# Normalized attention and a feed-forward block on one core: the first group's normalization in parts, two k scalings split over two engines, and two loads and two activations moved in their queues

## Chip, core, metric

One Trainium2 chip; the kernel runs on one of its cores. The metric is the device time of one execution in microseconds, as the median of several runs.

## What is computed

q, k and v have 8 batches, 12 heads, 448 tokens and a head dimension of 64, in float32. The attention output, 3584 tokens by 768, goes through an up-projection to 2048, a leaky activation with a slope per feature, and a down-projection to 768.

```python
def rmsnorm(x, g):
    rms = np.sqrt(np.mean(x * x, axis=-1, keepdims=True) + 1e-06)
    return x / rms * g
q_n, k_n = (rmsnorm(q, g_q), rmsnorm(k, g_k))
scores = (1.0 / np.sqrt(64)) * np.matmul(q_n, k_n.transpose(0, 1, 3, 2))
attn = softmax(scores)                       # over the keys
x = np.matmul(attn, v)                       # heads side by side: 3584 x 768
h = x @ w_in                                 # 3584 x 2048
g = np.maximum(h, 0.0) + alpha * np.minimum(h, 0.0)
out = g @ w_out                              # 3584 x 768
```

## The kernel before

A *group* `y` is one batch's four heads out of twelve: three groups to a batch (`G = 3`), 24 in all. Its q and k come as two tiles `nat` of 128 x 896 float32 (two halves of the heads on the two halves of the partitions; along a partition two heads `h`, seven token blocks `j` and 64 elements). Six such tiles exist, so three groups can be in the core at once. A group then goes through these steps:

- `load_qk` (L97): two DMAs for q and two for k, on SP's queue (half of those of groups 0 and 1 on ScalarE's).
- `square` (L141), on ScalarE for groups 0 and 1 and on GpSimd (POOL) after; `reduce` (L151), on VectorE; `root` (L159), two small ScalarE operations that make 1/rms; `scale` (L168), q or k times 1/rms, on VectorE for k of group 0 and q of groups 1 to 3 and on POOL for all others.
- `turn` (L188): for groups 0 to 5 fourteen TensorE transposes (`tps`) and two copies out of PSUM, `qT` and `kT`, the latter with the gains; from group 6 on two DMA transposes on SP's queue (`turn_dma`, L178) and only the gain on VectorE (L192).
- `score` (L225) and `soft` (L243), for each of the seven key blocks of a group: four or eight matmuls into one of two double banks `sc`, and one exponential of 128 x 896 on ScalarE, 1.0 us, into `expT`.
- `den`, `log`, `invert` and `attv`: the sums over the keys, their reciprocals by logarithm and exponential on ScalarE, the product with v, and `xT` on VectorE.

The feed-forward block is cut into pieces too. `up(b, ft)` (L344) makes one of 16 feature tiles of a batch: six matmuls into a PSUM bank `hT`, a ScalarE copy times the slope (`ah`, L354) and a VectorE maximum (`gT`, L355), which releases the bank. `down` (L357) is a chain of 16 matmuls into a bank `op`, a VectorE copy `osb` (L377) and two output DMAs on SP's queue. Feature tiles 0 to 3 of batch 0 are begun before the last third of the batch's attention is there (`begin`, L335): 0 and 1 in two single banks, 2 and 3 in the two halves of one shared tile (`hTb`).

The order of everything is written by hand: each engine runs its instructions in the order in which the program emits them. A list of *bursts* of two or three score tiles is laid out first; for every burst `n` the lists `prep`, `jobs`, `post` and `roots` say which loads, reduces, squares and roots go with it, `turns` which group is turned at it, and `gaps` which `up` and `down` pieces follow its scores. Burst `den_at[G - 1]`, the `lead`, is the one in which the attention of batch 0 ends and its up-projection starts; there `root` and `scale` of group 4 come after four `up` pieces. `spin` (L390) is a filler matmul whose result nobody reads; it keeps TensorE busy where it would wait. POOL's queue also issues the loads of v, w_in and w_out, among its squares and scales; w_out comes in four chunks of 768 KB. In the start, SP's queue issues groups 0 to 2 at once; groups 8 and 9 are loaded four bursts ahead of their reduces.

Of the kernel before, what the change touches and what calls it, by code (L numbers as in the profile page):

```python
# [9 lines left out]
FP32 = mybir.dt.float32  # L10
# [11 lines left out]
def kernel(  # L22
# [118 lines left out]
    def square(y, nm):  # L141
        src = nat[y, nm].rearrange("p h j d -> p (h j d)")
        sq = ld.tile([128, 2 * J, D], FP32, name="sq", tag="sq", bufs=4)
        sqf = sq.rearrange("p n d -> p (n d)")
        if y < 2:
            nc.scalar.activation(out=sqf, in_=src, func=AF.Square)  # L146
        else:
            nc.gpsimd.tensor_mul(out=sqf, in0=src, in1=src)  # L148
        sqs[y, nm] = sq

    def reduce(y, nm):  # L151
        if nm == "q":
            ss_t[y] = ld.tile([128, 2, 2, J], FP32, name="ss", tag="ss", bufs=4)
        nc.vector.tensor_reduce(  # L154
            out=ss_t[y][:, "qk".index(nm)].rearrange("p h j -> p (h j)").unsqueeze(2),
            in_=sqs[y, nm], axis=AXIS_X, op=ALU.add,
        )

    def root(y, nms="qk"):  # L159
        n = len(nms)  # L160
        at = "qk".index(nms[0])
        if at == 0:
            rr_t[y] = ld.tile([128, 2, 2, J], FP32, name="rr", tag="rr", bufs=4)
        rr, ss = rr_t[y][:, ds(at, n)], ss_t[y][:, ds(at, n)]
        nc.scalar.activation(out=rr, in_=ss, func=AF.Ln, scale=1.0 / D, bias=epsb[:, 0:1])
        nc.scalar.activation(out=rr, in_=rr, func=AF.Exp, scale=-0.5)

    def scale(y, nm):  # L168
        t = ld.tile([128, J, 2, D], FP16, name="qs", tag="qs", bufs=4)
        eng = nc.vector if (y, nm) in ((0, "k"), (1, "q"), (2, "q"), (3, "q")) else nc.gpsimd  # L170
        eng.tensor_mul(  # L171
            out=t.rearrange("p j h d -> p h j d"),
            in0=nat[y, nm],
            in1=rr_t[y][:, "qk".index(nm)].unsqueeze(3).broadcast_to((128, 2, J, D)),
        )
        qs[y, nm] = t

    def turn_dma(y):  # L178
        for nm in "qk":
# [8 lines left out]
    def turn(y):  # L188

        if y >= TD:  # L190
            t = qkT[y, "k"].rearrange("p j g c -> p (j g c)")
            nc.vector.tensor_scalar(  # L192
                out=t, in0=t, scalar1=gain[:, 0:1], scalar2=None, op0=ALU.mult
            )
            return
        if y <= G:
            ps = [psf.tile([128, 512], FP32, name="tps", tag="mm") for _ in "qk"]
        else:
            ps2 = psa.tile([128, 2, 512], FP32, name="tps2", tag="acc")
            ps = [ps2[:, 0], ps2[:, 1]]  # L200
        tps = [
            t[:, : S].bitcast(FP16).rearrange("p (j c) -> p j c", j=J) for t in ps
        ]
        for tp, nm in zip(tps, "qk"):
            for j in range(J):
                nc.tensor.transpose(  # L206
                    tp[:, j, :], qs[y, nm][:, j].rearrange("p h d -> p (h d)"), ident
                )
        for tp, nm in zip(tps, "qk"):
            t = att.tile([128, J, 2, 64], FP16, name=f"{nm}T", tag=f"{nm}T", bufs=4)  # L210
            o = t.rearrange("p j g c -> p j (g c)")
            if nm == "q" and y == 0:
                nc.scalar.copy(out=o, in_=tp)
            elif nm == "q":
                nc.vector.tensor_copy(out=o, in_=tp)
            else:
                nc.vector.tensor_scalar(
                    out=o, in0=tp, scalar1=gain[:, 0:1], scalar2=None, op0=ALU.mult
                )
            qkT[y, nm] = t  # L220
# [114 lines left out]
    def begin(ft):  # L335
# [5 lines left out]
            begun[2], begun[3] = t[:, 0], t[:, 1]  # L341
        up_part(begun[ft], 0, ft, 0, G - 1)

    def up(b, ft, spare=False):  # L344
        if b == 0 and ft in begun:
            hT = begun[ft]

            for n in {2: (2, 3), 3: ()}.get(ft, (ft,)):
                up_part(begun[n], 0, n, G - 1, G)
        else:  # L350
            hT = bank("hT", spare)
            up_part(hT, b, ft, 0, G)
        ah = ffn.tile([128, S], FP16, name="ah", tag="ah", bufs=3)
        nc.scalar.activation(out=ah, in_=hT[:, :S], func=AF.Copy, scale=alpha_sb[:, ft : ft + 1])  # L354
        nc.vector.tensor_max(out=gT[:, ft, ds((b & 1) * S, S)], in0=hT[:, :S], in1=ah)  # L355

    def down(b0, t, oh, jobs=(), spare=False):  # L357

# [31 lines left out]
    def spin(count, wide=True):  # L390

        ps = psf.tile([128, 512], FP32, name="spin", tag="mm")
        for _ in range(count):
            nc.tensor.matmul(  # L394
                out=ps[:, :S], lhsT=idle32[:, :128] if wide else ident,
                rhs=idle32 if wide else idle, start=True, stop=True,
            )
# [10 lines left out]
    m = 0  # L408
# [32 lines left out]
                last_in[y] = n  # L441
            m += 1
    NB = len(bursts)
    prep, post, roots = {}, {}, {}

    def at(n, f, *a):
        prep.setdefault(max(int(n), 0), []).append((f, a))
# [12 lines left out]
    for y in range(G, NG):  # L460

        early = y < G + 2
        if early:
            n = turn_at[y - 1] + 1
        elif y == G + 2:
            n = den_at[G - 1]
        elif y == 2 * G:
            n = turn_at[y] - 4
        elif y % G == 1:
            n = den_at[y - 4] - 1  # L470
        elif y % G:
            n = den_at[y - G]
        else:
            n = av_at[y - 4]
        at(n - (6 if early else 4 if y <= 3 * G else 5), load_qk, y)
        for nm in "qk":
            if y != 2 * G:
                after(n - 2, square, y, nm)
            if early:
                after(n, reduce, y, nm)  # L480
            else:
                jobs.setdefault(n, []).append((reduce, (y, nm)))
        roots[n + 1] = y
    for b in range(1, B):
        at(av_at[G * b] - 6, load_v, b)
# [87 lines left out]
    load_qk(1, True)  # L573
    load_qk(2)

    spin(3)
    spin(17, False)
    ct = psf.tile([128, 512], FP32, name="ct", tag="mm")
    nc.tensor.transpose(ct[:, : NF + 2], rows, ident32[: NF + 2, : NF + 2])
    spin(1)  # L580
    for nm in "qk":
        square(0, nm)
        reduce(0, nm)
    nc.vector.tensor_copy(out=cols, in_=ct[:, : NF + 2])
    for nm in "qk":
        root(0, nm)
        scale(0, nm)
    nc.vector.tensor_mul(
        out=gain, in0=cols[:, NF : NF + 1], in1=cols[:, NF + 1 : NF + 2]
    )  # L590
    square(1, "q")
    turn(0)
    square(1, "k")
    load_v(0)
    square(2, "q")
    for nm in "qk":
        reduce(1, nm)
    after(0, root, 1)
    for nm in "qk":
        after(0, scale, 1, nm)  # L600
    after(0, square, 2, "k")
    after(0, load_w_in, 0)
    for nm in "qk":
        after(2, reduce, 2, nm)
    after(5, load_w_in, 1)
    after(7, load_w_in, 2)
    after(8, load_w_in, 3)
# [1 line left out]
        after(first + (0, 0, 2, 4)[c], load_w_out, c)  # L609
    for nm in "qk":  # L610
        after(first, square, 2 * G, nm)
    roots[3] = 2

    since = 2
    for n in range(NB):
# [4 lines left out]
        lead = n == den_at[G - 1]  # L620
        first_tiles = tiles[: 2 if lead else split.get(n, 2)]
        for t in first_tiles:
            score(*t)
            if n == den_at[G - 1] - 1 and t == tiles[-1]:
                begin(0)
                begin(1)
            elif lead and t == tiles[0]:
                soft(*t)
                den(dens[n])
                attv(avs[n], 0, True, (log, invert))  # L630
            elif lead and t == tiles[1]:
                begin(2)
        plain = lead or n not in dens and n not in avs
        wait = plain and not lead and gaps[n] and gaps[n][0][0] is up
        if lead:
            begin(3)
        for t in tiles[:1] if wait else tiles[1:2] if lead else first_tiles:
            soft(*t)
        if n in dens and not lead:
            den(dens[n])  # L640
# [15 lines left out]
        if n in roots:  # L656
            y = roots[n]
            work = [(root, (y,)), (scale, (y, "q")), (scale, (y, "k"))]
            if lead:

                late = [(2, score, tiles[2]), (2, soft, tiles[2])]
            if lead or wait and y < TD:
                late += [(4 if lead else 1, f, a) for f, a in work]
            else:
                for f, a in work:
                    f(*a)
            if y >= TD:
                turn_dma(y)
# [28 lines left out]
        for k, (f, a) in enumerate(gaps[n]):  # L697
            spare = k in spare_at
            if f is down:
                down(*a, jobs.pop(n, ()), spare)  # L700
            else:
                f(*a, spare)
                done += 1
                if n in jobs and not (lead and done < 4):
                    g, c = jobs[n].pop(0)
                    g(*c)
                    if not jobs[n]:
                        del jobs[n]
                while late and done == late[0][0]:
                    _, g, c = late.pop(0)  # L710
                    g(*c)
        if not gaps[n] and n in turns:
            turn(turns[n])
        for _, g, c in late:
            g(*c)
# [36 lines left out]
```

## Time and profile before

| | |
|---|---|
| median of 6 runs | 433.4 us (431.95 to 434.43) |
| the profiled execution | 433.73 us, of which the span of its trace is 431.9 us |
| TensorE (PE), loads of its weights (PEld) | busy 417.1 and 216.3 us |
| ScalarE (ACT), VectorE (DVE), GpSimd (POOL) | busy 279.0, 203.2 and 175.2 us |
| DMA | 53.85 MB moved, 125 GB/s over the span |
| exponential `expT`, 168 of them | 1004 ns each |
| POOL `qs` and `sq`, 44 each | 1761 and 1677 ns each |
| VectorE `ss` (reduce), 48 of them | 1077 ns each |

Busy time is the sum of an engine's instructions. TensorE's includes the fillers. Where the text gives a moment (13.43), it is in microseconds from the start of the span.

### The profile page before, as it was taken

How to read it: one execution, taken by the hardware profiler on the slowest of the kernel's cores; microseconds unless marked ns; L12 is line 12 of the kernel's file. 1: busy time of each engine (PE TensorE's matmuls, PEld its weight loads, DVE VectorE, ACT ScalarE, POOL GpSimd, SP SyncE). 2: the span in 40 equal slices, each digit the busy share in tenths (PEclk: the TensorE clock that was granted, in tenths of full speed). 3: DMA queues.
4: the chain of work that ended last, by engine and by line, in shares of the span. 5: the costliest groups of instructions: out<-in, count | busy, mean ns of one | idle time of the engine just before them, and what ended most of it. 6: DMA issues, size and time to landing. Idle time of an engine off the chain costs nothing.

```text
span 431.9 us, 11487 instructions
## 1 busy us (share of the span) xinstructions
PE 417.1 (97%) x4964; PEld 216.3 (50%) x4964; DVE 203.2 (47%) x304; ACT 279.0 (65%) x385; POOL 175.2 (41%) x133
## 2 busy tenths in 40 slices
PE   8789899899999999999999999999999999999996
PEld 3344344454455445544555445544555445555564
DVE  3755764455545463545444463545453353233421
ACT  4997888677976677767667577757757577132300
POOL 5799696393184407380283506371163000000000
PEclk9999999999999999999999999999999999999999
DMA  8999899999669824878059833774073300211133
GB/s 195 235 220 219 154 212 147 241 192 212 129 109 193 180 80 63 171 146 185 20 96 196 174 115 61 152 149 116 20 119 87 77 1 21 56 38 32 24 73 75
DMA packets 70387, 53.85 MB, mean 125 GB/s; under 512 B 37424, under 2 KB 70336, under 8 KB 70336
## 3 DMA queue, kind: packets, MB, share of 16 engines
q1 hardware_dynamic: 55536, 40.19, 43.0%
q0 software_dynamic: 13984, 11.81, 19.1%
q10 hardware_dynamic: 816, 1.11, 1.1%
q8 instruction: 39, 0.64, 0.6%
q14 instruction: 12, 0.10, 0.1%
HBM read 45.62 MB, written 11.01 MB: 131 GB/s over the span
## 4 chain that ended last, share of the span: by engine, by line
PE 86%; ACT 5%; DMA 4%; DVE 3%; POOL 1%; issue 1%
PE op L365 27%; PE hT L327 21%; PE hTa L327 11%; PE sc L232 7%; PE opa L365 6%; PE av L261 4%; PE dn L261 4%; DMA w_out_sb<-in_moe_w_out_dram 4%; ACT expT L246 3%; PE spin L394 2%; PE avb L261 2%; DVE ss L154 1%; PE tps L206 1%; DVE gT L355 1%; POOL sq L148 1%; DVE osb L377 1%
## 5 line engine op out<-in xcount | busy, mean ns | idle before, releaser
L246 ACT ACTIVATE expT<-sc,expb 128x896 f16<-128x896 f32 x168 | 161.5, 1004 | 36.8 <-PE sc L232 35.8
L171 POOL TENSOR_TENSOR qs<-nat,rr 128x896 f16<-128x896 f32 x44 | 76.7, 1761 | 148.6 <-issue 79.0
L365 PE MATMUL op<-w_out_sb,gT 128*128 128x384 f16 (+1 forms) x752 | 126.5, 323 | 1.0 <-DMA w_out_sb<-in_moe_w_out_dram 1.0
L365 PEld LDWEIGHTS <-gT 128*128 128x128 f16 x912 | 85.8, 98 | 66.6 <-issue 14.0
L327 PEld LDWEIGHTS <-w_in_sb 128*128 128x128 f16 x768 | 73.2, 98 | 75.8 <-issue 11.5
L327 PE MATMUL hT<-xT,w_in_sb 128*128 128x448 f16 x510 | 107.1, 353 | 2.8 <-DVE gT L355 2.2
L354 ACT ACTIVATE ah<-hT,cols 128x448 f16<-128x448 f32 x85 | 53.7, 634 | 44.6 <-PE hT L327 44.6
L355 DVE TENSOR_TENSOR gT<-hT,ah 128x448 f16<-128x448 f32 x85 | 52.8, 623 | 51.0 <-ACT ah L354 51.0
L148 POOL TENSOR_TENSOR sq<-nat 128x896 f32<-128x896 f32 x44 | 72.9, 1677 | 9.3 <-DMA nat<-in_q_dram 6.8
L377 DVE COPY osb<-op 128x384 f32<-128x384 f32 (+1 forms) x47 | 25.8, 548 | 86.7 <-PE op L365 86.7
L232 PE MATMUL sc<-qT,kT 64*32 64x448 f16 (+1 forms) x1092 | 53.2, 356 | 4.3 <-ACT expT L246 2.8
L154 DVE TENSOR_REDUCE ss<-sq 128x14 f32<-128x896 f32 x48 | 50.5, 1077 | 9.5 <-ACT sq L146 5.9
L327 PE MATMUL hTa<-xT,w_in_sb 128*128 128x448 f16 x246 | 53.2, 352 | 0.0
L354 ACT ACTIVATE ah<-hTa,cols 128x448 f16<-128x448 f32 x41 | 26.0, 634 | 31.3 <-PE hTa L327 31.3
L355 DVE TENSOR_TENSOR gT<-hTa,ah 128x448 f16<-128x448 f32 x41 | 25.6, 623 | 26.0 <-ACT ah L354 26.0
L232 PEld LDWEIGHTS <-kT 64*32 64x32 f16 (+1 forms) x1092 | 15.0, 93 | 36.2 <-issue 30.8
L365 PE MATMUL opa<-w_out_sb,gT 128*128 128x384 f16 x160 | 27.7, 326 | 0.6 <-DVE xT L312 0.6
L312 DVE TENSOR_TENSOR xT<-av,rden 128x896 f16<-128x896 f32 x16 | 17.4, 1090 | 17.9 <-PE av L261 14.2
L261 PEld LDWEIGHTS <-vt 64*32 64x32 f16 (+1 forms) x1260 | 18.9, 94 | 13.2 <-issue 2.2
L261 PE MATMUL dn<-expT,ones 64*32 64x448 f16 (+1 forms) x812 | 24.2, 350 | 0.9
L261 PE MATMUL av<-expT,vt 64*32 64x448 f16 (+1 forms) x812 | 24.1, 349 | 0.0
L278 ACT ACTIVATE rden<-dn 128x896 f32<-128x896 f32 x16 | 14.5, 907 | 7.3 <-PE dn L261 7.3
(45 smaller groups left out, 160.7 us busy)
## 6 DMA issues: line engine op xcount, KB each, us to landing
out_dram<-osb SPq DMA_DIRECT2D x109, 96.0 KB, 2.3
nat<-in_q_dram SPq DMA_DIRECT2D x46, 224.0 KB, 5.4
nat<-in_k_dram SPq DMA_DIRECT2D x46, 224.0 KB, 6.7
vt<-in_v_dram POOLq DMA_DIRECT2D x16, 336.0 KB, 6.9
w_in_sb<-in_moe_w_in_dram POOLq DMA_DIRECT2D x12, 256.0 KB, 8.1
w_out_sb<-in_moe_w_out_dram POOLq DMA_DIRECT2D x4, 768.0 KB, 12.4
nat<-in_q_dram ACTq DMA_DIRECT2D x2, 224.0 KB, 4.9
nat<-in_k_dram ACTq DMA_DIRECT2D x2, 224.0 KB, 6.2
```

What stands on the lines that cost most here:

```text
L148: nc.gpsimd.tensor_mul(out=sqf, in0=src, in1=src)
L154: nc.vector.tensor_reduce(out=ss_t[y][:, "qk".index(nm)].rearrange("p h j -> p (h j)").unsqueeze(2), in_=sqs[y, nm], axis=AXIS_X, op=ALU.add,)
L171: eng.tensor_mul(out=t.rearrange("p j h d -> p h j d"), in0=nat[y, nm], in1=rr_t[y][:, "qk".index(nm)].unsqueeze(3).broadcast_to((128, 2, ...
L232: nc.tensor.matmul(out=sc[ds(64 * g + m * c, m), par, :S].rearrange("p (j c) -> p j c", j=J), lhsT=kT[ds(64 * par, 64), j, g, ts(c, m)], r ...
L246: nc.scalar.activation(out=expT[y][:, j], in_=scs[y, j][:, :, :S], func=AF.Exp, scale=QK_SCALE, bias=expb[:, 0:1],)
L261: nc.tensor.matmul(out=accs[g][ds(m * h, m), :S], lhsT=weights(g, y, par, ts(c, m), j), rhs=expT[y][ds(64 * g, 64), j, par, :], start=(j = ...
L312: nc.vector.tensor_mul(out=x, in0=av[:, :, :S], in1=r)
L327: nc.tensor.matmul(out=hT[:, :S], lhsT=w_in_sb[:, g * G + i, ts(ft, 128)], rhs=xT[b][:, g, i, :], start=(i == 0 and g == 0), stop=(i == G ...
L354: nc.scalar.activation(out=ah, in_=hT[:, :S], func=AF.Copy, scale=alpha_sb[:, ft : ft + 1])
L355: nc.vector.tensor_max(out=gT[:, ft, ds((b & 1) * S, S)], in0=hT[:, :S], in1=ah)
L365: nc.tensor.matmul(out=ops[c][:, :PW], lhsT=gT[:, ft, ts(t, 128)], rhs=w_out_sb[:, ft, ds(oh * OH + c * PW, PW)], start=(ft == 0), stop=(f ...
L377: nc.vector.tensor_copy(out=o[:, ts(c, PW)], in_=ops[c][:, :PW])
```

## The change

- The first group. `square`, `reduce`, `root`, `scale` and `turn` of group 0 are written out in parts: q is squared and reduced head by head (2 x 448), with one root and one scale on POOL; k is squared, reduced, rooted, scaled on VectorE, transposed and copied in token blocks 0 to 2 and 3 to 6. The scores of the first blocks stand ahead of the transposes of the others. The copy `qT` of this group moves from ScalarE to VectorE; one filler ahead of the first transposes goes and one at the start.
- Groups 1 and 2. The square of group 1's k moves from ScalarE to POOL. `root` and `scale` move to just before the last exponential of bursts 1 and 4, and the scaling of k is split by heads, one half on VectorE and one on POOL. The turns of both groups move to just ahead of scores (1,0) and (1,6), which is one tile later than before.
- The shared tile. `ah` and `gT` of feature tiles 2 and 3 of batch 0 are held until those of tile 4 have been emitted. In the lead, `root` and `scale` of group 4 come after two `up` pieces and not four; the second reduce of group 5 goes to the next burst's list.
- Loads. Groups 8 and 9 are loaded after burst `den_at[3]`; on SP's queue they come behind two outputs, the transposes of group 7 and two more outputs, where they came ahead of all of these.

```diff
     def scale(y, nm):
         t = ld.tile([128, J, 2, D], FP16, name="qs", tag="qs", bufs=4)
-        eng = nc.vector if (y, nm) in ((0, "k"), (1, "q"), (2, "q"), (3, "q")) else nc.gpsimd
+        eng = nc.vector if nm == "q" and 0 < y <= G else nc.gpsimd
...
+    def part_scale(nm, j, n, eng, y=0, h=None):
+        if (y, nm) not in qs:
+            qs[y, nm] = ld.tile([128, J, 2, D], FP16, name="qs", tag="qs", bufs=4)
+        hs, m = (slice(0, 2), 2) if h is None else (slice(h, h + 1), 1)
+        eng.tensor_mul(
+            out=qs[y, nm][:, j, hs].rearrange("p j h d -> p h j d"),
+            in0=nat[y, nm][:, hs, j],
+            in1=rr_t[y][:, "qk".index(nm), hs, j].unsqueeze(3).broadcast_to((128, m, n, D)),
+        )
...
+        if b == 0 and ft in (2, 3):
+            held.append((hT, ft))
+            return
+        units = [(hT, ft)]
+        if b == 0 and ft == 4:
+            prelu(units, b)
+            units = held
+        prelu(units, b)
...
-        at(n - (6 if early else 4 if y <= 3 * G else 5), load_qk, y)
+        if y in (2 * G + 2, 3 * G):
+            after(den_at[G], load_qk, y)
+        else:
+            at(n - (6 if early else 4 if y <= 3 * G else 5), load_qk, y)
...
-                jobs.setdefault(n, []).append((reduce, (y, nm)))
+                jobs.setdefault(n + (y == G + 2 and nm == "k"), []).append((reduce, (y, nm)))
...
-    spin(3)
+    spin(2)
     spin(17, False)
...
-    spin(1)
-    for nm in "qk":
-        square(0, nm)
-        reduce(0, nm)
+    K0 = 3
+    both, full, lo, hi = slice(0, 2), slice(0, J), slice(0, K0), slice(K0, J)
+    for h in range(2):
+        part_square("q", slice(h, h + 1), full, nc.scalar)
+    for h in range(2):
+        part_reduce("q", slice(h, h + 1), full)
+    part_root("q", full)
+    part_scale("q", full, J, nc.gpsimd)
+    part_square("k", both, lo, nc.scalar)
+    part_square("k", both, hi, nc.scalar)
+    part_reduce("k", both, lo)
+    part_reduce("k", both, hi)
+    part_root("k", lo)
+    part_scale("k", lo, K0, nc.vector)
+    part_root("k", hi)
+    square(1, "q")
     nc.vector.tensor_copy(out=cols, in_=ct[:, : NF + 2])
...
+    part_turn("q", range(J))
+    part_turn("k", range(K0))
+    part_copy("q", full, nc.vector)
+    part_copy("k", lo, nc.vector)
+    load_v(0)
     square(1, "k")
-    load_v(0)
+    part_scale("k", hi, J - K0, nc.vector)
+    reduce(1, "q")
     square(2, "q")
+    after(0, part_turn, "k", range(K0, J))
+    after(0, part_copy, "k", hi, nc.vector)
+    after(0, reduce, 1, "k")
+    mid[1] = 1
...
-    roots[3] = 2
+    mid[4] = 2
...
+            if t in ((1, 0), (1, J - 1)):
+                turn(1 + (t[1] > 0))
             score(*t)
...
+            if n in mid and t == tiles[-1]:
+                root(mid[n])
+                scale(mid[n], "q")
+                part_scale("k", full, J, nc.vector, mid[n], 0)
+                part_scale("k", full, J, nc.gpsimd, mid[n], 1)
             soft(*t)
...
-                late += [(4 if lead else 1, f, a) for f, a in work]
+                late += [(2 if lead else 1, f, a) for f, a in work]
```

## The prediction

> **What bounds the kernel now.** I read the 40 slices first, for which engine is full where; then the waits, for what stops TensorE; then the chain in order of time; then the timeline around each place that the change touches.
>
> ```profile
> PE   8789899899999999999999999999999999999996
> ...
> ACT  4997888677976677767667577757757577132300
> ...
> PEclk9999999999999999999999999999999999999999
> DMA  8999899999669824878059833774073300211133
> ```
>
> A slice is 10.8 us. From the tenth on TensorE is full, so there a microsecond is won only by removing matmuls, and the change removes none of those that compute. Time is to be had in the first nine slices. There PE's digits still flatter it, since its fillers (spin, L394) count as busy. In the windows from 0 to 100 us PE is idle 10.4 us in all; from 100 to 300 us it is idle 0.6 us. DMA is full nearly throughout those first nine slices as well.
>
> ```profile
> PE hT L327 <- DVE gT L355: 2.2, 2, 1.7
> ...
> PE op L365 <- DMA w_out_sb<-in_moe_w_out_dram: 1.0, 1, 1.0
> ```
>
> Two of TensorE's waits after the start: it waits for VectorE to release an up-projection bank (the 1.7 us one at 49.0) and for the last chunk of w_out (at 86.3). The chain shows what comes before:
>
> ```profile
> 12.25 0.70 DVE kT L217
> 12.95 0.04 issue
> 12.99 0.41 PE sc L232 x4
> 13.40 0.02 issue
> 13.43 1.91 ACT expT L246 x2
> ...
> 17.64 0.38 PE sc L232 x4
> 18.02 0.51 PE tps L206 x7
> 18.54 0.02 issue
> 18.56 0.62 DVE qT L215
> 19.18 0.63 DVE kT L217
> ...
> 67.86 18.40 DMA w_out_sb<-in_moe_w_out_dram
> 86.27 0.04 issue
> 86.31 1.46 PE op L365 x8
> ```
>
> The first exponential starts at 13.43. From there to 36.6 ScalarE is the bound: sixteen exponentials at a step of 0.91 us (two take 1.91 with the tail of the last), with roots of 0.48 between them, and one gap of 0.47 at 21.4. Only two score banks exist, so a score waits for the exponential two before it.
>
> **What the Trainium skill says.** "SBUF — State Buffer", section "Who interferes with whom": a VectorE instruction with two SBUF inputs and a GpSimd one that reads SBUF exclude each other. The trace agrees: POOL's scale takes 1.69 us at 8.95 and 2.59 at 15.87, where VectorE's 1.09 us scale starts at 15.83. "DMA: Bandwidth & Descriptors", section "Queues, rings and completion order": each DMA engine goes round the queues packet by packet, so SP's loads slow POOL's. The trace agrees: the last w_out chunk takes 18.4 us to land beside loads and transposes, another one 9.1. "TensorE: Matmul & The Clock Gate", section "What's actually happening": an idle window of about 3.4 us halves the clock. The trace shows 1.00 throughout and no idle stretch of that length; no run here shows the other case.
>
> **Part 1, the first group.** Now: q lands at 5.52; square 0.95, reduce 1.09; q's root waits behind k's square and ends at 8.87; POOL's scale ends at 10.64; k's side ends with kT at 12.95. After, the durations of the halves are interpolated between the 14-element root (0.21) and the 896-element square (0.95): half a square 0.58, half a reduce 0.58.
> - q: squares 5.52 to 6.56, the second reduce ends at 7.2, root (0.54) 7.76, ahead of k's square. POOL's scale (1.69) 7.84 to 9.53, 1.1 earlier. One spin fewer before it and none behind ct let PE take it at once.
> - k: squares 7.76 to 8.85 in two parts; reduces to 8.83 and 9.5; root of tokens 0 to 2 at 9.40; their scale on VectorE to 10.05; cols and gain to 10.35; qT, now on VectorE instead of ScalarE, 0.62 to 10.98; kT of three token blocks (0.68 x 3/7 = 0.3) to 11.3; score 11.35; first exponential about 11.8.
> - So 1.6 us earlier. ScalarE also loses the copy (0.91) and the square of k of group 1 (0.95), both of which stood before 13.43. That square goes to POOL behind v's two DMA issues (1.37): 10.9 to 12.6; its reduce ends at 14.6, root at 15.1. Behind it on POOL wait group 2's squares and w_in's issues; their users (21.8 and 35.1 before) have slack.
>
> **Part 2, turns one tile later.** Group 1's transposes stood behind score (0,5); now they stand behind (0,6). From the end of the exponential that frees that score's bank to the first exponential of group 1 the trace of before takes 2.7 us (17.60: score 0.38, transposes to 18.56, qT, kT to 19.81, score, 20.30). Before, three exponentials cover it (2.7); after, two (1.8). New gap 0.9. A spin (0.95 from issue to the next score) now stands between (1,0) and (1,1): another 0.35. The gap of 0.47 goes, since the reduces end before ScalarE asks. The same at group 2's turn, with the spin before (2,0): 0.5. Scaling k by halves (VectorE 0.6 beside POOL 0.85 instead of 1.69 on POOL, stretched to 2.59) brings qs from 18.46 to about 17.4, but the transposes wait for score (0,6) anyway: worth nothing on its own. Sum: 1.6 - 0.9 - 0.35 + 0.47 - 0.5 is 0.3; followed tile by tile (root of group 3 at 29.2 against 29.64) it is 0.4. I take 0.4; the ends are 0 and 1.6 (turns hidden).
>
> **Part 3, shared-tile outputs later.** Feature tile 4 goes through ScalarE and VectorE ahead of 2 and 3. Its gT ends at 46.8 instead of 48.99, and the 1.7 us wait at 49.04 goes. Late next: gT of 2 and 3 to 47.95, group 5's first reduce (1.08) to 49.0, gT 5 to 49.6, the second reduce to 50.6, the root in order on ScalarE to 51.15, ah 6, gT 6 at 52.4 (51.77 before). Tile 8 needs that bank: it ends at 53.7 against 54.0. So 0.3 of the 1.7 is kept (ends 0 and 1.7). The root of group 4 comes 1.7 earlier, and POOL, back to back from 47.4 to 68.8, moves forward; w_out's last issue goes from 67.86 to about 66.5.
>
> **Part 4, loads of groups 8 and 9 later.** On SP the eight loads (1.83 MB) leave the place behind group 6's transposes (68.3 to 77.9) and come behind two outputs, group 7's transposes and two more outputs. What they stood beside speeds up: group 6's kT lands at 77.27 now and holds VectorE, behind it xT, behind that the bank for PE at 78.77 (0.61). And w_out's chunk, 18.4 us now, takes 9 to 12 as the others: landed at about 77, needed at 85: the 1.01 goes. Sum 1.6. The cost: group 7's transposes start when its scale ends (74) and issue by 77; two outputs; the loads issue from about 78 to 83 and land (1.83 us each at the 250 GB/s of this stretch) at 82.5, 84.8, 86.7, 88.5, against 80.15, 84.1, 86.8 and before 88.5 now. VectorE waits in order for their squares, with an output copy, kT and xT behind. I price that at nothing within the slack, 0.6 us as worked out under the third rival, and at up to 4 without it.
>
> **The rest.** Two spins fewer: filler; from 8.6 to 9.5 PE stands idle, far under the window named above; 0 to 1 us. Group 5's second reduce a burst later: already in the order above. From 100 us on nothing moves but the start.
>
> Sum: 0.4 + 0.3 + 1.6 = 2.3. The profiled execution took 433.73 (span 431.9, 1.8 around it), 0.3 above the median of 433.4. 433.73 - 2.3 is 431.4; set against the median, **431.1**.
>
> **Rivals.**
> 1. *The turns cost nothing* (0.2): the whole 1.6 of the first group survives and more of the 1.7. For it: group 1's scaled k is ready early. Against: the order on PE is fixed, and (1,0) can't run before kT. 1.6 + 0.6 + 1.6 = 3.8: 429.6.
> 2. *Head and lead gain nothing, and the transfers bind* (0.22): DMA is full from 2 to 48 us, the earlier v load (POOL at 9.5 instead of 10.6) delays group 2's q, on which POOL already waits to 13.54, and the turns eat the rest. Only part 4 stays, less late loads: 0.8: 432.6.
> 3. *Slower: group 8's k lands late* (0.14). VectorE takes reduce q, reduce k, output copy (0.56), kT (0.45 to 0.70), xT (1.07) in order; PE needs that xT at 92.93 - 2.3 = 90.6, so the reduce must end by 88.3, and nat k must land by 85.5 (square 1.68, reduce 1.09): 0.6 us after my 84.8. Each microsecond beyond is lost. Issued at 80, it loses when it takes over 5.5 us; all such loads have a median of 5.8 and here they reached 14.4. At 9.5 us it costs 4: 433.4 + 4 - 2.3 = 435.1.
>
> **How the numbers follow.** The case of the sum has 0.44; it gives 430 to 432.1. About 0.3% (1.3 us) is what a measurement of this kernel can tell from no change. Faster by more, under 432.1: the sum's case and the first rival, with a little of the second, 0.67. Within it: most of the second and the near end of the third, 0.2. Slower, over 434.7: 0.13. The range leaves out 0.1 below and 0.1 above: 428.8 to 434.6.
>
> **What would show it.** After: first exponential at 11.8; ScalarE idle near 19 for about 0.9 and near 27 for 0.4; group 3's root at about 29.2; no PE wait of 1.7 us before the seventh up tile but one of about 1 for the ninth; qT and kT of group 6 landed before VectorE asks; no op wait for w_out; VectorE's reduce of group 8 waiting for POOL near 85 and PE not. The prediction is wrong if the head's 1.6 arrives whole at 30 us, or if PE waits for xT or an output bank near 90.

## The result and the profile after

The changed kernel takes 434.55 us (median of 35 executions, 431.88 to 439.52); the kernel before, beside it, 433.48 us (72 executions). The ratio is 1.0018, with a 95% interval of 1.0003 to 1.0033: no gain, and a small loss. Executions more than 1.5% above the fastest of their kernel are left out of all ratios and of the table by clock below; they are few, except where POOL issues group 8's loads, with nine of 22 (438.4 to 444.4 us; of the kernel before, beside it, two of 27). The profiled execution took 435.54 us, its span 433.4, against 433.73 and 431.9 before.

Most of the parts went as the sum has them, and TensorE stood 2.5 us ahead at 85 us. At 105 us it was 1.6 us behind. First the slices of the changed kernel, the same rows as before:

```profile
PE   8789899979999999999999999999999999999996
...
ACT  5898888758877577758757577757757577132300
...
PEclk9999999989999999999999999999999999999999
DMA  8999999999559743788049742775064300211133
```

One digit in each of two rows tells the story. The ninth slice, 87 to 98 us, now has a 7 on PE and an 8 for the granted clock; before, the clock had 9 in all forty slices. The waits of the changed kernel (engine, line and tile, what it waited for: us in total, times, the longest):

```profile
DVE ss L154 <- POOL sq L148: 8.6, 3, 5.7
...
PE sc L294 <- DVE kT L256: 2.3, 1, 2.3
...
PE hT L389 <- DVE gT L418: 1.2, 2, 0.8
```

TensorE's waits for w_out and for an up-projection bank of 1.7 us are gone from the list. A new one of 2.3 us stands in it, on VectorE's kT, and above it what VectorE was waiting for: POOL's squares, which stood waiting for their loads. The chain in order of time (start, us, what) shows how these hang together:

```profile
80.86 7.23 DMA nat<-in_k_dram
...
88.24 1.69 POOL sq L148
...
90.96 0.55 DVE osb L458
...
92.32 0.57 PE sc L294 x8
92.89 2.36 PE hT L389 x6
95.25 1.68 PE hTa L389 x6
...
104.86 1.24 PE hT L389 x6
106.10 1.14 PE hTa L389 x6
```

Group 8's k is issued at 80.86 and lands at 88.08. Then come POOL's square, VectorE's reduce (to 91.04) and, behind that reduce in VectorE's order, the output copy, kT of group 7, and only then the score. The two lines after the score cost a second time: the same groups of six matmuls that take 1.24 and 1.14 us at 105 took 2.36 and 1.68 here. Windows of two microseconds (length, busy time of PE, PEld, DVE, ACT and POOL with counts, granted clock, DMA share, GB/s) show why:

```profile
90.00:92.00 2.00, 0.00 (x0) 0.00 (x0) 2.00 (x3) 0.54 (x2) 1.66 (x2) 1.00 1.08 289
92.00:94.00 2.00, 1.68 (x12) 0.65 (x13) 2.00 (x3) 1.01 (x1) 2.00 (x3) 0.71 1.07 221
94.00:96.00 2.00, 2.00 (x7) 0.83 (x6) 1.72 (x3) 0.68 (x3) 2.00 (x3) 0.50 0.87 150
```

TensorE is empty for 2.33 us, to 92.32, and the clock then falls to a half. Idle 2.33 and slow matmuls 1.66 (2.36 + 1.68 less 1.24 + 1.14) make 4.0 of the 4.1 us between "2.5 ahead" and "1.6 behind". From 150 to 420 us the windows of both kernels agree.

In the head, three of ScalarE's exponentials (start, us, in brackets the idle time before and what ended it):

```profile
19.51 1.01 ACT L308 ACTIVATE expT<-sc,expb 128x896 f16<-128x896 f32 x1 [0.88 <-PE sc L294]
20.77 1.01 ACT L308 ACTIVATE expT<-sc,expb 128x896 f16<-128x896 f32 x1 [0.26 <-PE sc L294]
...
27.07 1.91 ACT L308 ACTIVATE expT<-sc,expb 128x896 f16<-128x896 f32 x2 [0.34 <-PE sc L294]
```

The first exponential, not shown, starts at 11.60 instead of 13.43, 1.83 us earlier. The turns of groups 1 and 2 give back the 0.88, 0.26 and 0.34 shown here, as a turn one tile later has to. And in the lead TensorE's timeline has two new gaps where the wait of 1.7 us was:

```profile
48.17 0.38 PE L294 MATMUL sc<-qT,kT 64*64 64x448 f16 x4 [0.90 <-ACT expT L308]
...
51.34 1.30 PE L389 MATMUL hT<-xT,w_in_sb 128*128 128x448 f16 x6 [0.77 <-DVE gT L418]
```

### The profile page after: what moved, and what is told of

Its sections match the earlier page's. It is cut to its first block, busy times and chain, and to the rows that moved or that the text cites. A ratio compares the mean times of both kernels' runs of the same rounds, so it can differ in the third digit from the quotient of the medians.

```text
span 433.4 us, 11492 instructions
## 1 busy us (share of the span) xinstructions
PE 417.1 (96%) x4960; PEld 216.4 (50%) x4960; DVE 206.5 (48%) x311; ACT 278.3 (64%) x387; POOL 176.3 (41%) x134
## 4 chain that ended last, share of the span: by engine, by line
PE 83%; ACT 5%; DVE 4%; issue 2%; POOL 2%; DMA 2%; SPq 1%; ACTq 1%; POOLq 0%
PE op L446 26%; PE hT L389 22%; PE hTa L389 11%; PE sc L294 7%; PE opa L446 6%; PE dn L323 4%; PE av L323 4%; ACT expT L308 2%; PE avb L323 2%; DMA nat<-in_k_dram 2%; DVE ss L154 1%; DVE gT L418 1%; DVE osb L458 1%; POOL qs L171 1%; POOL sq L148 1%
## 5 line engine op out<-in xcount | busy, mean ns | idle before, releaser
L171 POOL TENSOR_TENSOR qs<-nat,rr 128x896 f16<-128x896 f32 x41 | 69.6, 1719 | 140.9 <-issue 93.2
L148 POOL TENSOR_TENSOR sq<-nat 128x896 f32<-128x896 f32 x45 | 75.7, 1703 | 12.6 <-DMA nat<-in_q_dram 10.2
L154 DVE TENSOR_REDUCE ss<-sq 128x14 f32<-128x896 f32 x46 | 48.5, 1077 | 8.6 <-POOL sq L148 8.6
```

The costliest lines, as they stand in the source:

```text
L154: nc.vector.tensor_reduce(out=ss_t[y][:, "qk".index(nm)].rearrange("p h j -> p (h j)").unsqueeze(2), in_=sqs[y, nm], axis=AXIS_X, op=ALU.add,)
L171: eng.tensor_mul(out=t.rearrange("p j h d -> p h j d"), in0=nat[y, nm], in1=rr_t[y][:, "qk".index(nm)].unsqueeze(3).broadcast_to((128, 2, ...
```

## The experiments

In the expectations, A is the theory that the late landing of group 8's k is what the change pays for. B, as its rival, says that what is won early is lost again whatever the loads do. D is the theory that the new start puts the granted clock at risk, so that its gain arrives only in part of the executions. Ratios are to the kernel before, run on the same chip. The changed kernel was not run again beside these, so a comparison with it goes over two ratios.

### A: taking the late loads away, and having nothing but them

**Loads back at their place, the rest of the change kept:**

```diff
-        if y in (2 * G + 2, 3 * G):
-            after(den_at[G], load_qk, y)
-        else:
-            at(n - (6 if early else 4 if y <= 3 * G else 5), load_qk, y)
+        at(n - (6 if early else 4 if y <= 3 * G else 5), load_qk, y)
```

> The changed kernel with the loads of groups 8 and 9 back in their old place on SP's queue. Theory A (late k: VectorE waits in order for group 8's k, TensorE then stands 2.3 us idle near 90 us and runs about 1.7 us slow behind it): both losses go, the start's 1.5 us stays won, w_out's last chunk is waited for again (1.0 us, or more since TensorE arrives 1.5 earlier): 431.5 to 433. Theory B (what is won in the start is given back later whatever the loads do, because DMA is full): 434.5, with another wait in place of this one.

Measured: 433.23 us, ratio 1.0001 (0.9977 to 1.0024). No stall near 90, and a time just above A's range and below B's. But no gain is left either: head and lead together bring nothing in the median. Its profiled execution shows another loss, which comes back below: a pause of 2.95 us inside a chain of `av` matmuls at 74.3, for nothing that the profile names, with the clock at 0.54 and 0.61 in the four microseconds behind it.

**The move of the loads alone**, the same lines put into the kernel before:

> The kernel before with nothing changed but the place of the loads of groups 8 and 9. Theory A: no wait for w_out (1.0 us won), group 6's kT earlier by up to 0.6, but group 8's k lands near 89.5, TensorE waits 2 to 3 us near 92 for kT behind VectorE's reduce, and its clock drops for 1.7 us: 435.5 to 437. Theory B: 431.8 to 432.5, the loads only help.

Measured: 435.29 us, ratio 1.0036 (1.0014 to 1.0057), slower. That is 0.2 below A's range and far above B's. With the old start and the old lead the stall is the same. From TensorE's rows in the timeline of this kernel:

```profile
93.03 0.57 PE L232 MATMUL sc<-qT,kT 64*64 64x448 f16 x8 [2.02 <-DVE kT L192]
93.54 2.42 PE L327 MATMUL hT<-xT,w_in_sb 128*128 128x448 f16 x6
```

Idle 2.02, then six matmuls in 2.42 us. The move of the loads costs by itself about what the whole change loses (the two intervals overlap).

**Squares that need not wait.** In the changed kernel the squares of groups 8 and 9 read group 7's tiles, which are in the core; all loads and instructions stay, so that what is left is the time with squares that find their data.

```diff
         src = nat[y, nm].rearrange("p h j d -> p (h j d)")
+        if y in (8, 9):
+            src = nat[7, nm].rearrange("p h j d -> p (h j d)")
```

> The changed kernel, all loads in its places, but the squares of groups 8 and 9 read group 7's tiles, which have long landed (their norms are then group 7's). Theory A: VectorE's reduces no longer wait for the late loads, kT and xT of group 7 come in time, no idle TensorE near 90, no lower clock behind it: 3 us or so below the changed kernel, 431 to 432. Theory B: 434.5.

Measured: 432.03 us, ratio 0.9981 (0.9954 to 1.0008), 2.5 us under the changed kernel by the medians and 1.6 by the two ratios: A's case. The window in which that one had an empty TensorE:

```profile
90.00:92.00 2.00, 2.00 (x18) 0.88 (x17) 1.89 (x3) 0.54 (x2) 1.90 (x2) 1.00 1.20 224
```

The run isn't quite the changed kernel less its stall: with the squares POOL's next load of v comes 11 us earlier too (82.28 instead of 93.75), and near 78 TensorE still waits 0.5 and 0.6 us for VectorE.

**Group 8's loads from POOL's queue.** POOL has nothing to do from 74.95 to 84.75 but wait for that very q. It issues the loads itself, behind its scales of group 7:

```diff
-            (nc.scalar if y < 2 and g else nc.sync).dma_start(
+            (nc.gpsimd if y == 2 * G + 2 else nc.scalar if y < 2 and g else nc.sync).dma_start(
```

> The changed kernel with group 8's four loads issued by POOL instead of SP: they come right behind POOL's scales of group 7 (which end at 74.95 and after which POOL waits 9.8 us for group 8's q), so about 3 us ahead of their place on SP's queue, and still behind the issue of group 6's transposes. Theory A: k of group 8 lands by 85.5, the wait of 2.3 us near 91 goes, the clock there stays at 1.00; what group 9's late loads cost (about 1 us near 97) may remain; median 432.0 to 433.4 us, ratio 0.997 to 1.000, executions with the full granted clock 431.3 to 432.6. Rival: the loads now go beside group 7's DMA transposes (73.3 to 76.8), which hold the DMA engines almost alone, so that nothing lands earlier and kT of group 7 comes later: k of group 8 lands at 87 to 88, TensorE waits 1 to 3 us near 91 as before; 434 to 435.5.

Measured: 432.87 us (median of the 13 executions that the ratio uses; over all 22 it is 434.23), ratio 1.0002 (0.9978 to 1.0026), against 432.35 for the kernel before on this chip. The expected median is met by the 13 alone, and the time doesn't show a gain. Whether the new place of issue brings the nine long executions no run has shown. The trace shows the mechanism. POOL's two squares of group 8 and TensorE's rows:

```profile
82.43 1.67 POOL L148 TENSOR_TENSOR sq<-nat 128x896 f32<-128x896 f32 x1 [4.76 <-DMA nat<-in_q_dram]
...
84.49 1.68 POOL L148 TENSOR_TENSOR sq<-nat 128x896 f32<-128x896 f32 x1 [0.38 <-DMA nat<-in_k_dram]
...
89.20 0.57 PE L294 MATMUL sc<-qT,kT 64*64 64x448 f16 x8
89.70 1.31 PE L389 MATMUL hT<-xT,w_in_sb 128*128 128x448 f16 x6
```

k landed by 84.5, a microsecond inside the limit of 85.5. The squares start at 82.43 and 84.49 instead of 84.75 and 88.24, the score at 89.20 instead of 92.32 without a wait, and the six matmuls take 1.31. Group 9's loads hold nothing up here either. The span of this execution is 429.2 us, 4.2 under that of the changed kernel and 2.7 under that of the kernel before: in this one execution the forecast gain is there. A holds, for the stall near 91: in this profile three microseconds of issue time decide it.

### What the stall is made of: waiting, clock, and group 9 behind it

The wait near 91 filled with two matmuls that nobody reads, so that the clock has no reason to fall:

```diff
+            if t == (2 * G + 1, 0):
+                fill = pss.tile([128, 2, 512], FP32, name="fill", tag="sc")
+                for _ in range(2):
+                    nc.tensor.matmul(out=fill[:, 0, :S], lhsT=idle32[:, :128], rhs=idle32, start=True, stop=True)
             score(*t)
```

> The changed kernel with two filler matmuls (0.95 us each) ahead of group 7's first score, in the idle time near 90 us; they go into a free score bank. Theory A with the clock as a consequence of the wait: the wait for kT stays (its end near 92.3), the six up matmuls behind it take 1.3 us instead of 2.4, and the time is 1.5 to 1.7 lower than that of the changed kernel: 432.9. Theory C (the lower clock in that window is chance and has nothing to do with the wait): the clock is as often low as before, 434.5 or a little more.

Measured: 435.68 us, ratio 1.0029 (1.0001 to 1.0057). The clock stays at 1.00 from 90 to 100, but nothing is won, against the 432.9 of theory A. The profile doesn't test the clock as it was meant to. In this execution the clock had fallen near 12, and TensorE reaches the place at 91.9 instead of 90.0; kT is ready at 92.76, and the fillers, which last to 93.5, outlive the wait. So theory C, that the fall has nothing to do with the wait, isn't ruled out by this run. What its timeline shows is the next link, as late:

```profile
97.57 2.62 PE L389 MATMUL hT<-xT,w_in_sb 128*128 128x448 f16 x12 [1.09 <-DVE osb L458]
```

VectorE's output copy, at 96.97, stands behind the two reduces of group 9, whose loads are late too. In the changed kernel this copy ends at 95.72 and TensorE, slowed, comes to it at 96.8. At full clock it would have come near 95.1 (an estimate, with the 2.3 us that the same twelve matmuls take in the run with POOL's queue), so the slow clock hid some 0.6 us of a second wait.

That group 9 alone does this is shown by moving only its load:

```diff
-        if y in (2 * G + 2, 3 * G):
+        if y == 3 * G:
```

> The changed kernel with group 8 loaded at its old place and only group 9 late. Theory A: group 8's squares and reduces come in time, no idle TensorE near 90; w_out lands beside one group's loads instead of two, so its wait is 0 to 1 us; group 9 is needed later: 430.7 to 432. Theory B: 434.5.

> Again the changed kernel with group 8's load at the old place and group 9's late, for a profile that can be read. Theory A: no stall near 90, the squares of group 8 wait for nothing, w_out waits less than 0.5 us; time 433.0 to 433.8, profile near 431.5 to 433 in span. Rival (the load of group 9 alone, landing after 86 us, is late for its squares): TensorE waits 0.5 to 1.5 us for osb near 97 as where the wait near 90 was filled; then the gain of w_out goes there.

Measured: 433.34 us, ratio 0.9991 (0.9964 to 1.0019), and again 433.60, 0.9995 (0.9965 to 1.0025). The first left no profile that can be read (its profiled execution took 851 us), and its time lies between the two theories. The second shows no stall at 91, a wait of 1.16 us for w_out where A had under 0.5, and near 97:

```profile
97.27 2.62 PE L389 MATMUL hT<-xT,w_in_sb 128*128 128x448 f16 x12 [1.30 <-DVE osb L458]
```

The rival of that expectation holds: group 9's late load costs 1.3 us there. A part of A's account had been too simple, in that group 8 was to pay for everything.

### Group 8 early instead of late

If late is bad, ahead of group 6's transposes should be good: `load_qk(8)` just before `turn_dma(6)`, group 9 late.

```diff
-        if y in (2 * G + 2, 3 * G):
+        if y == 2 * G + 2:
+            pass
+        elif y == 3 * G:
             after(den_at[G], load_qk, y)
...
+            if y == 2 * G:
+                load_qk(2 * G + 2)
             if y >= TD:
                 turn_dma(y)
```

In the changed kernel:

> The changed kernel with group 8 loaded ahead of group 6's transposes on SP's queue (its buffers are free from 55.8 us, SP is idle from 48 to 61), group 9 where the change put it. Theory A (late k of group 8 blocks VectorE, TensorE stands and slows): group 8 lands before 70, its reduces stand at once at their turn, no wait for kT near 90; group 9's reduces may still be waited for, under 1 us. 2 to 3 us below the changed kernel: 431.5 to 432.5. Theory B (the gain is lost in any case to full DMA): 434 to 434.5, with w_out or v late in its place.

and in the kernel before, with the same move:

> The kernel before with its own start and its own lead; of the change only what is useful in the move of the loads: group 9 is issued behind the den of group 2, and group 8 goes ahead of group 6's transposes instead of behind the output stage. Theory A (the late landing of group 8's k is what the change pays for): nothing stalls near 90, the reduces of group 8 find their squares, the wait for w_out (1.0 us) is gone; 432.0 to 432.9 us, ratio 0.997 to 0.999. Rival: 0.9 MB issued ahead of the transposes makes kT of group 6 land later, and TensorE waits about 2 us near 81 with VectorE idle over 3 us ahead of that kT, as where group 8 was loaded early with the new start; then 433.5 to 434.5. The start is the old one, so the granted clock should be 1.00 from 10 to 30 us; if it falls there too, the new start isn't the cause of the loss of clock.

Measured: 434.71, ratio 1.0021 (0.9997 to 1.0046), and 435.80, ratio 1.0059 (1.0037 to 1.0082), slower. Theory A's times failed for both. The rival of the second had the mechanism, though the time lies above its range too. No stall near 90 in either, but kT of group 6 is now late. In the second:

```profile
78.56 1.31 DVE L192 TENSOR_SCALAR kT<-kT,gain 128x896 f16<-128x896 f16 x1 [3.92 <-DMA kT<-qs]
79.92 0.38 PE L232 MATMUL sc<-qT,kT 64*64 64x448 f16 x4 [2.16 <-DVE kT L192]
```

TensorE's wait moved from 91 to 80; in the first it is 2.16 us as well, to 81.0. The old place of the loads, behind group 6's transposes and ahead of group 7's, is a place between two late users.

### D: the start and the granted clock

**The new start alone** (loads at the old place, maxima, lead and reduces as before):

> The changed kernel with the loads of groups 8 and 9 at the old place and the lead as before (max of each tile at once, root and scale after the fourth tile, reduces of tile G+2 not shifted): the new start is all that is left of the change. Theory D (the head's 1.5 us is kept only in executions in which the clock holds in the first 30 us, and is partly lost in others): 432.9 to 433.6 us, ratio 0.999 to 1.001, as with start and lead together (433.2). Rival: the start gains its 1.5 us in most executions and the new lead costs it again: 431.8 to 432.4, ratio 0.996 to 0.998.

Measured: 432.99 us, ratio 1.0000 (0.9975 to 1.0025), as D has it and not its rival. In its profiled execution the clock falls where the changed kernel's did not:

```profile
12.00:14.00 2.00, 2.00 (x10) 0.72 (x9) 0.75 (x2) 1.45 (x2) 2.00 (x2) 0.50 1.09 230
14.00:16.00 2.00, 1.94 (x14) 0.53 (x11) 1.38 (x2) 1.54 (x4) 0.83 (x1) 0.73 1.21 217
```

The first exponential starts at 11.54, and yet the seventh up tile starts at 48.52, where it starts at 48.53 with the old start (group 8 early in the kernel before, 49.04 in before itself): the head's gain is gone. Further on this execution pauses for 0.95 us in a chain of `av` matmuls and waits 2.15 us for w_out, where the kernel before waits 1.01; so the clock is not all that it lost.

Eight profiles have the new start with nothing added to it. In five of them the clock fell in the first 30 us: to about 0.5 near 12 us with the filled wait, with group 8 early, with resident squares and with the start alone, and to 0.57 at 24 to 28 us with group 9 late (with group 8 early it fell a second time there). In three it stayed at 1.00: the changed kernel, the loads back, and group 8 from POOL. The three profiles with the old start (before, loads alone, group 8 early in before) kept it.

What goes with the fall near 12 us can be read from the same eight profiles. First the changed kernel, then the one with the wait filled, whose start is the same program:

```profile
4.68 4.77 PE L475 MATMUL spin<-gT,ident 128*128 128x448 f16 x17
...
9.54 0.90 PE L224 MATMUL tps<-ident,qs 128*128 128x128 f16 x10
```

```profile
4.68 3.39 PE L475 MATMUL spin<-gT,ident 128*128 128x448 f16 x17
...
9.68 0.82 PE L224 MATMUL tps<-ident,qs 128*128 128x128 f16 x10 [0.71 <-POOL qs L213]
```

The seventeen fillers end at 9.45 in one and at 8.07 in the other. In the four profiles in which the clock fell near 12 they took 3.4 to 3.7 us, and TensorE stood idle for 1.6 to 2.0 of the 3.1 us from 8.0 to 11.1. In the four others they took 4.3 to 4.8 us, and it stood idle for 0.7 to 1.2. Why the same fillers take longer in some executions no run shows. Nor does the idle time decide alone: with the old start, two of the three profiles (loads alone, group 8 early in before) have 2.0 to 2.1 us of it in the 3.3 us ahead of the first score, and their clock held. What the start does is shown by the counts. On one chip, side by side, 13 of 21 executions of the new start alone have a mean clock below 0.998, and 3 of 37 of the kernel before.

**Filling the start:** five narrow fillers more ahead of the first transposes, three behind them.

```diff
-    spin(17, False)
+    spin(22, False)
...
+    fill = pss.tile([128, 2, 512], FP32, name="fill", tag="sc")
+    for _ in range(3):
+        nc.tensor.matmul(out=fill[:, 0, :S], lhsT=ident, rhs=idle, start=True, stop=True)
```

> The changed kernel with eight narrow fillers more in the start: five before the transpose of the small vectors and three behind group 0's first transposes (into a free score bank), so that TensorE has no idle time of 0.7 us between 8 and 11.3 us. Theory D (with its fillers gone, TensorE's clock is halved near 12 us in part of the executions, which costs 1.4 us of the start): the clock in the start is 1.00 and the median falls by 0.3 to 1.0 us against the changed kernel, to about 433.9. Without theory D: 434.5 to 434.8.

With group 8 early as well:

> Group 8 loaded ahead of group 6's transposes and the start filled as in the run with fillers. Theories A and D together: 431 to 432, below the kernel before by about 0.4%. Theory B: 434.

Measured: 435.74, ratio 1.0070 (1.0038 to 1.0103), and 437.66, ratio 1.0108 (1.0070 to 1.0145): both slower, where D had 433.9 and 431 to 432. The clock held from 8 to 20 us in the first and then fell to 0.62 and 0.53 between 20 and 24; in the second it fell at 16 and stayed near 0.5 to 26. This remedy fails, so gaps in the first ten microseconds are not the whole of it; what exactly makes the clock fall in one execution and not in the next stays open.

### The executions sorted by their clock

Every execution comes with the mean granted clock over its span. The fall behind the stall, two windows of 2 us at 0.71 and 0.50, takes 1.6 us or 0.4% off it. Sorted by whether it is at least 0.998:

| kernel | executions | clock 0.998 or more: number, median us | below: number, median us |
|---|---|---|---|
| before | 164 | 145, 432.96 | 19, 435.77 |
| changed | 34 | 18, 433.88 | 16, 435.45 |
| loads alone | 22 | 13, 434.24 | 9, 436.02 |
| loads back | 19 | 10, 432.60 | 9, 435.15 |
| new start alone | 21 | 8, 432.29 | 13, 433.19 |
| group 9 late (both) | 33 | 19, 432.07 | 14, 434.54 |
| group 8 early, changed | 14 | 6, 432.62 | 8, 435.06 |
| group 8 early, before | 9 | 1, 434.69 | 8, 436.00 |
| squares resident | 14 | 7, 431.03 | 7, 433.01 |
| group 8 from POOL | 13 | 9, 432.60 | 4, 433.99 |
| wait filled | 21 | 11, 434.63 | 10, 436.98 |
| start filled | 12 | 3, 434.99 | 9, 436.86 |
| group 8 early, start filled | 6 | none | 6, 437.66 |

This grouping was made after the fact, the groups are small and they come from different chips: the kernel before, at full clock, has medians of 432.34 to 433.09 in the four sets that are taken together here. Half a microsecond is not resolved in it. It says two things beyond that. The executions that lose clock are 0.9 to 2.8 us longer in the median. And with the kernel before they are one in nine, with each of the others, which have the new start or open a gap of 2 us, three to ten in ten.

No version here beats the kernel before by more than its interval.

## Why the prediction was wrong

Forecast 431.1 and faster; measured 434.55 and slower. The number is still inside the stated range, at its slow end (434.6); the direction is wrong. By its own steps:

- **Part 1**, first exponential 1.6 earlier: 1.83. Right.
- **Part 2**, turns: gaps of 0.9, 0.35 and 0.5, measured 0.88, 0.26 and 0.34. Net 0.4 at group 3's root; measured 0.67 (28.97 against 29.64). Right. By 36 us it is 1.47, mostly because TensorE's pause of 0.62 at 37.0 in the profile of before has no counterpart. I had not seen that pause, which names no cause; that part of the gain is luck.
- **Part 3**, lead: 0.3 of 1.7 to be kept; measured nothing (1.47 ahead at 36 and at 53.3). The new wait for the ninth up tile is there, 0.77 for the 1 foretold. The wait of 0.90 for an exponential ahead of it was not in the working.
- **Part 4, what it wins**: w_out's wait of 1.0 went, and so did the 0.61 for a bank. Right. That TensorE stood 2.50 ahead at 85.2, against 2.3 foretold, is in part luck: the head and lead brought 1.47 for the 0.7 foretold, and part 4 only 1.03, mostly because the changed kernel's own profile has a pause of 0.47 at 74.4. In the executions with full clock, resident squares are 1.6 us under the loads at their old place (431.03 against 432.60). That is the 1.6 of the sum, but no check of it, since their profile still has the 0.61.
- **Part 4, what it costs: "I price that at nothing within the slack".** This is the step that failed. The condition was stated correctly: k of group 8 must land by 85.5. The landing was sized at 84.8 and was 88.08, so the term put at nothing was 2.33 us of idle TensorE and a fall of the clock behind it. My first issue was right (78 against 78.16). The landing assumed 250 GB/s from there and one tile after the other. Over 78.2 to 88.2 us, in 40 equal slices, the DMA engines show this:

```profile
DMA  9999900008999999999999989999999999999999
GB/s 187 212 340 251 60 0 7 9 9 175 289 223 362 393 426 366 344 230 208 222 229 230 215 186 251 252 194 201 229 201 215 208 244 201 208 201 244 201 230 215
```

  For 1.3 us at the start, near 79.2 to 80.5, next to nothing is moved; what held the engines there no run has shown. The profile of before has such a pause too, 1.25 us from 87.25, beside group 7's transposes (issued from 82.67 to 87.76), so one could have been counted. Then, for most of the stretch, they move some 215 GB/s. And the stretch moved 2.17 MB in all, where q and k of group 8 are 0.92: what was issued before and behind them, outputs and group 9's loads, went along beside them and not after them. Each of the three is against the estimate. A margin of 0.7 us (the prediction has 0.6, a slip), on loads whose like took 5.8 us in the median over the profile before, and 11.0 between 60 and 92 us with up to 14.4, was not a margin.
- **The rival that happened** had 0.14: group 8's k late, "each microsecond beyond is lost". 88.1 less 85.5 is 2.6, and the idle time was 2.33. It gave 435.1 in its example, and 434.55 was measured; that they are near is luck, since its rule gives 433.7 for a landing at 88.1, without the clock's fall. The mechanism and the order of instructions behind it were as written, though TensorE stopped at kT, one ahead of the xT named. With such a margin its chance was too small.
- **The clock.** I put "no idle stretch of that length" beside the section "What's actually happening" of "TensorE: Matmul & The Clock Gate" in the Trainium skill and so priced gaps at nothing, and "two spins fewer" at 0 to 1. But the section also says that the window of about 3.4 us is free-running, and another of that page, "A second HAM failure mode: psum-queue depth-cycling", that short idle times between groups of matmuls can make the clock swing. Here 2.33 us of idle were followed by half the clock for about 3 us, and in the start, in four profiles, two or three gaps of 0.6 to 1.0 us in a row were. Reading the idle time as a threshold was the error. Its size: 1.66 us in the profile behind the stall, and in the median over executions 0.56 (434.44 over all 34, 433.88 with full clock), where the kernel before has 0.0 to 0.2.
- **Smaller slips.** From 13.43 to 36.6 ScalarE has 21 exponentials, not sixteen, and a chance of 0.13 above 434.7 doesn't go with one of 0.1 above 434.6. Neither bears on the forecast.

Put in a row from the executions with full clock: the start wins 0.7 (432.29 against 432.96), the lead costs 0.3 (432.60 against 432.29), the loads win 1.6, their lateness costs 2.9 (433.88 against 431.03), and the clock costs some 0.4 more than before. That is 1.3 slower; the medians of the direct comparison differ by 1.07. The first four terms add up by the way they are formed, and across chips; only the two of the loads stand clear of what the table resolves, and by the ratios the lateness is 1.6.

## What to carry to other kernels

When a load is moved later, its latest landing time, worked out from the in-order queue behind its first user, is worth more than the wait that it relieves: take the slowest landing that the profile shows at such a place and not the bandwidth's quotient, and if the margin is under a microsecond, price the miss as likely. An engine that idles ahead of the transfer's consumer can issue it earlier, three microseconds here, which took the stall out of the profile but showed no gain in the time. Gaps on TensorE can carry a second price, a halved clock behind them, and here they carried it in a share of the executions, so a single profile can show a gain that the median doesn't have.

## What the runs showed of the hardware that was not expected

- A gap of 2.0 to 2.3 us on TensorE, amid full work, was followed by a clock of 0.50 and about 3 us of slow matmuls in the changed kernel and with the loads alone. With group 8 early, the same gap of 2.16 us near 80 was followed by 1.00 in two profiles (new start and old) and by 0.50 in the third (start filled). So it is not the length alone.
- The same start instructions ran at 1.00 in some executions and at 0.5 for 2 to 4 us in others. In the eight profiles the fall near 12 us goes with an early end of the fillers ahead of it (8.07 to 8.38 us, against 8.96 to 9.45).
- TensorE stops inside runs of matmuls for 0.46 to 2.95 us with no wait in the profile: at the seventh up-projection matmul in the kernel before (0.62) and with the loads alone (0.46), and at the 45th `av` matmul of one chain in the changed kernel (0.47), with the wait filled (0.77), with the start alone (0.95) and with the loads back (2.95); other profiles have no pause there. The place is fixed in the program and the length varies. The page counts 39 packets and 0.64 MB on an "instruction" queue, so fetching the program through busy DMA engines would fit; no run tests it.
- VectorE's multiplication of kT by the gain takes 0.45 us while POOL is idle (at 75.3 in the changed kernel) and took 0.85 and 1.31 beside POOL's squares (at 91.4 there, at 78.6 with group 8 early in the kernel before). No run isolates it.
